# A depthwise-convolution and MLP kernel: the first tap's product on GpSimd, and other half steps for the visits

## Chip, core and metric

The kernel runs on one core of a Trainium2 chip. The metric is the device time of one execution in microseconds (us); lower is better. A core has five engines that run their own instruction queues in order: TensorE (PE in the profile; its weight loads PEld), VectorE (DVE), ScalarE (ACT), GpSimd (POOL) and SyncE (SP). DMAs are issued by SP, ACT and POOL queues.

## What is computed

With S = 2048 positions, D = 448 channels and F = 1792, all in float32:

```python
xn = layernorm(q)
# branch A: short causal convolution of k (4 taps), times v, long causal convolution, gate
k_shift = sum(k_pad[:, t:t + S] * shift_k[:, 3 - t] for t in range(4))
kv = k_shift * v
y = irfft(rfft(kv, 2 * S) * rfft(ssm_k, 2 * S))[:S] + kv * ssm_D
A = xn * y
# branch B: dense, Mish, dense
B = mish(xn @ w1 + b1) @ w2
out = q + A + B
```

## The kernel before

**Branch B sets the rhythm.** The 2048 positions are 8 chunks c of 256, the 1792 hidden channels 7 pairs p of 128-wide blocks; (c, p) is pair i = 7c + p. Each pair takes two half steps. In the even one, s = 2i, TensorE runs `g1_mm(i)` (line 556, 22 matmuls with split operands); in the odd one `mish(i)` (ScalarE, line 564; then `split`, whose line 98 is a ScalarE cast to `ach` and line 99 a VectorE subtraction to `acl`), and TensorE runs `g2_mm(i - 2)` (lines 588 to 590, 12 matmuls, which accumulate a chunk in two PSUM tiles). When a chunk's last pair is through, `g2_evac` (line 595, VectorE, two operations) empties those two tiles into Q; the next chunk's first `g2_mm` writes the same two. For chunk 1 that is half steps 32 and 33, for chunk 2 half steps 45 and 47.

**Branch A lies between.** The long convolution is a Fourier transform in two stages. The first stage works on 8 groups g of 256 positions, once for the filter h and once for kv. A "visit" at half step t is `f1_mm` (line 166, 16 small matmuls into the PSUM tiles pq and pr), then `f1_fold` (ScalarE copies pr, line 172; VectorE adds and subtracts, line 176, twice), then, three half steps later, `f1_out` (line 187, two DMAs to the scratch tensors Dh or Dkv). From half step 60 on the second stage ("octets", lines 255 to 321) reads Dh and Dkv back.

**kv itself** is made on VectorE by `taps(g, u)` for u = 0 to 3, spread over the half steps ahead of the visit: u = 0 is one product k times tap (line 209, 128x896); u = 1 and 3 are two half products (lines 212 and 214) and an addition (219); u = 2 has its product made on GpSimd by `taps_pool` (line 202) and only added here (219); after u = 3 the sum is multiplied with v (222). `taps_pool(g + 1, 2)` is put behind the visit of g, ahead of its fold; it begins with a VectorE memset of one element (line 201) which makes GpSimd wait until VectorE has come that far. The k tiles come from `k_load` (line 192, SP, four buffers), v from `v_load` (196).

**LayerNorm of chunks 3 to 7**: `nt_stats` at half step NT_STATS[c] (27, 41, 53, ... ; ScalarE lines 478 to 480, GpSimd 481 and 482, and a DMA to MR, line 486, on POOL), `nt_row` (line 489: SP loads MR, broadcast to all partitions), `nt_norm` (line 495, VectorE, a pair of operations) and `nt_split` (ScalarE 502, VectorE 503), twice for each chunk.

**What sets the order.** The program is written out half step by half step: `at(t, ...)` puts work ahead of the matmuls of half step t, `after(t, ...)` behind them, in the order of registration; every engine, and every DMA queue, then takes its own part of that one order strictly in turn. H_AT and KV_AT hold the half steps of the visits of h and kv. For kv, with d the distance to the visit before:

```python
    for g, t in enumerate(KV_AT):
        d = t - (KV_AT[g - 1] if g else t - 6)
        at(t - d - (3 if g > 1 else 2), k_load, g)
        at(t - d - 1, v_load, g)
        for u in range(4):
            after(t - (2 if g else 1) - d + d * u / 4, taps, g, u)
        at(t, f1_mm, KV, g, "kv")
```

Of the kernel before, what the change touches and what calls it, by code (L numbers as in the profile page):

```python
# [14 lines left out]
S, D, F = 2048, 448, 1792  # L15
# [7 lines left out]

G2_LAG = 2
H_HEAD = 1
H_AT = {2: 6, 3: 9, 0: 12, 4: 16, 5: 20, 6: 26, 7: 32}
KV_AT = (24, 29, 34, 39, 44, 50, 56, 60)
POOL_H = {20: (0, 2)}
OCT_AT = (66, 3)
I2_AT = {100: ((6, 7, 0, 1), 92, (95, 97, 98, 99), (0, 2, 0, 1)),  # L30
# [20 lines left out]
def tile_kernel(ctx: ExitStack, tc, q, qT, k, v, sk, hT, sD, head, w1, w2, c_g, c_gi, c_i2, out):  # L51
    nc = tc.nc
    V = nc.vector
# [67 lines left out]
    def dv(n=1):  # L121
        for _ in range(n):
            if drip:
                drip.pop(0)()
# [4 lines left out]
    def at(slot, fn, *args):  # L129
        plan.setdefault(int(slot), []).append((fn, args))  # L130
# [7 lines left out]
    skb = sp1.tile([128, 4, D], F32, name="skb")  # L138
    HT, KR, VT, KV, PP, PS, ST, SD = {}, {}, {}, {}, {}, {}, {}, []

    def xt():
        return sp1.tile([128, 2, D], F32, name="x", bufs=7)
# [61 lines left out]
    def taps(g, u):  # L204
        if (g, u) in PP:
            o = PP.pop((g, u))
        elif u % 2 == 0:
            o = xt()
            V.tensor_mul(o, KR[g - u // 2], skb[:, u:u + 1].to_broadcast([128, 2, D]))
        else:  # L210
            o = xt()
            V.tensor_mul(o[:, 0], KR[g - (u + 1) // 2][:, 1], skb[:, u])
            dv()
            V.tensor_mul(o[:, 1], KR[g - u // 2][:, 0], skb[:, u])
        dv()
        if u == 0:
            KV[g] = o
        else:
            V.tensor_add(KV[g], KV[g], o)  # L219
            dv()  # L220
        if u == 3:
            V.tensor_mul(KV[g], KV[g], VT.pop(g))
            dv()
# [430 lines left out]

    for g, t in H_AT.items():
        if g != H_HEAD:
# [10 lines left out]
    for g in range(-2, 0):  # L667
        at(12, k_load, g)
# [7 lines that stand above are left out]
        if g + 1 < NO:  # L676
            after(t, taps_pool, g + 1, 2)
        after(t, f1_fold, g, "kv")
        (at if t % 2 or g == NO - 1 else after)(t + (3 if g < NO - 1 else 2), f1_out, Dkv, g, "kv")
# [216 lines left out]
```

## Time and profile before

| | |
|---|---|
| median of 3 runs | 357.84 us (356.28 to 359.15) |
| the profiled execution: time, span | 356.18 us, 354.4 us |
| mean granted TensorE clock | 0.998 |
| busy PE, PEld | 349.8 us (99%), 288.6 us (81%) |
| busy DVE, ACT, POOL | 282.1 us (80%), 160.7 us (45%), 72.6 us (20%) |
| the stretch 48 to 186 us: PE, DVE, POOL busy | 138.00, 119.08, 31.74 us |

A row of the profile's groups gives line, engine, operation, out<-in tiles, shapes, count, then busy time and mean duration in ns, then the idle time ahead of it and what ended most of it. A row in order of time starts with the start and the duration in us ("x2" puts two operations together); what stands in brackets is the idle time ahead. The duration of a VectorE row is a little longer than the distance to the next start: two rows of 1.09 that don't depend on each other start 1.00 apart.

### The profile page before, as it was taken

The page shows a single profiled execution, that of the slowest core. Times are in us where ns is not written, and L with a number is a line of the kernel's source. Part 1 is how long each engine was busy: PE and PEld are TensorE (multiplying, and loading weights), DVE is VectorE, ACT ScalarE, POOL GpSimd, SP SyncE. Part 2 cuts the span into 40 slices and gives each one's busy share as a digit, 9 for nine tenths or more (in the row PEclk, how much of TensorE's full clock was granted, in tenths as well). Part 3 has the DMA queues.
Part 4 walks back from the last instruction along what each step waited for, and adds up shares of the span by engine and source line. Part 5 has one row for each costly group of instructions (what it writes and reads, how often), then busy time and mean ns, then how long its engine had stood idle before and what let it go on. Part 6 is the DMA issues. An engine that isn't in the chain of part 4 may idle for free.

```text
span 354.4 us, 7525 instructions
## 1 busy us (share of the span) xinstructions
PE 349.8 (99%) x3098; PEld 288.6 (81%) x3098; DVE 282.1 (80%) x375; ACT 160.7 (45%) x310; POOL 72.6 (20%) x85
## 2 busy tenths in 40 slices
PE   8999999999999999999999999999999999999996
PEld 2988888888888989889887568658757699979795
DVE  5899748998999998979539869868985963788943
ACT  5967552347343643364232732423724333354480
POOL 3046002822220250212000120110310116040030
PEclk9999999999999999999999999999999999999999
DMA  7999977848769356652969489679756467989076
GB/s 251 366 339 353 401 277 182 338 131 236 212 178 314 128 150 176 219 163 36 298 187 365 149 307 298 229 243 372 263 144 254 105 173 261 407 334 277 25 116 143
DMA packets 30835, 83.27 MB, mean 235 GB/s; under 512 B 3153, under 2 KB 15954, under 8 KB 30802
## 3 DMA queue, kind: packets, MB, share of 16 engines
q1 hardware_dynamic: 21986, 47.78, 39.8%
q0 software_dynamic: 4928, 22.95, 20.4%
q10 hardware_dynamic: 3888, 12.08, 12.5%
q8 instruction: 24, 0.39, 0.4%
q14 instruction: 9, 0.07, 0.1%
HBM read 54.34 MB, written 28.45 MB: 234 GB/s over the span
## 4 chain that ended last, share of the span: by engine, by line
PE 97%; DMA 1%; SPq 0%; DVE 0%; issue 0%
PE pg L556 24%; PE pg L590 13%; PE pg L588 13%; PE pg L589 13%; PE pa L556 6%; PE pq L556 5%; PE pq L166 4%; PE pa L310 3%; PE pr L556 3%; PE pr L255 3%; PE pq L255 3%; PE pp L556 2%; PE pa L255 1%; DMA x<-in_head_dram 1%; PE pp L364 1%; PE pb L556 1%
## 5 line engine op out<-in xcount | busy, mean ns | idle before, releaser
L588 PE MATMUL pg<-w2h,ach 128*128 128x448 f32 x222 | 80.7, 363 | 0.0
L590 PE MATMUL pg<-w2h,acl 128*128 128x448 f32 x222 | 80.6, 363 | 0.0
L589 PE MATMUL pg<-w2l,ach 128*128 128x448 f32 x222 | 80.5, 362 | 0.0
L99 DVE TENSOR_TENSOR acl<-a,ach 128x512 fp32r<-128x512 f32 x56 | 38.9, 694 | 33.0 <-ACT ach L98 32.8
L556 PE MATMUL pg<-XH,w1h 128*128 128x256 f32 x264 | 52.7, 283 | 0.0
L564 ACT ACTIVATE a<-pg,b1t 128x256 f32<-128x256 f32 x66 | 27.8, 472 | 51.8 <-PE pg L556 40.9
L556 PEld LDWEIGHTS pg<-XH,w1h 128*128 128x128 f32 x264 | 41.3, 188 | 8.2 <-issue 6.3
L588 PEld LDWEIGHTS pg<-w2h,ach 128*128 128x128 f32 x222 | 41.6, 187 | 4.4 <-issue 1.4
L589 PEld LDWEIGHTS pg<-w2l,ach 128*128 128x128 f32 x222 | 41.7, 188 | 2.4
L590 PEld LDWEIGHTS pg<-w2h,acl 128*128 128x128 f32 x222 | 41.7, 188 | 2.4
L556 PE MATMUL pg<-XL,w1h 128*128 128x256 f32 x264 | 42.9, 277 | 0.0
L176 DVE TENSOR_TENSOR st<-pq,st 128x896 f32<-128x896 f32 x32 | 34.9, 1089 | 4.8 <-ACT st L172 4.2
L98 ACT CAST ach<-a 128x512 fp32r<-128x512 f32 x56 | 34.8, 621 | 8.2 <-PE pg L589 6.7
L556 PEld LDWEIGHTS pg<-XL,w1h 128*128 128x128 f32 x264 | 35.9, 188 | 0.0
L556 PE MATMUL pg<-XH,w1l 128*128 128x256 f32 x198 | 33.5, 278 | 0.0
L202 POOL TENSOR_TENSOR x<-kr,skb 128x896 f32<-128x896 f32 x8 | 17.0, 2128 | 72.1 <-PE pr L166 25.7
L321 POOL DMA_DIRECT2D E<-qe x14 | 8.8, 631 | 92.7 <-ACT qe L264 92.7
L556 PEld LDWEIGHTS pg<-XH,w1l 128*128 128x128 f32 x198 | 27.6, 188 | 0.0
L219 DVE TENSOR_TENSOR x<-x 128x896 f32<-128x896 f32 x24 | 26.2, 1091 | 1.1 <-POOL x L202 0.4
L172 ACT COPY st<-pr 128x896 f32<-128x896 f32 x16 | 14.5, 908 | 15.9 <-PE pr L166 14.7
L564 ACT ACTIVATE a<-pa,b1t 128x256 f32<-128x256 f32 x16 | 6.7, 472 | 20.8 <-PE pa L556 20.7
L166 PE MATMUL pq<-x,con 32*64 32x448 f32 x128 | 15.9, 560 | 0.1
(191 smaller groups left out, 645.8 us busy)
## 6 DMA issues: line engine op xcount, KB each, us to landing
Dkv<-st ACTq DMA_DIRECT2D x16, 448.0 KB, 5.5
ah<-Dh SPq DMA_DIRECT2D x8, 896.0 KB, 8.4
av<-Dkv SPq DMA_DIRECT2D x8, 896.0 KB, 9.6
e<-E POOLq DMA_DIRECT2D x8, 896.0 KB, 7.3
E<-qe POOLq DMA_DIRECT2D x14, 448.0 KB, 7.1
kr<-in_k_dram SPq DMA_DIRECT2D x10, 448.0 KB, 6.0
Dh<-st ACTq DMA_DIRECT2D x10, 448.0 KB, 6.9
x<-in_v_dram SPq DMA_DIRECT2D x8, 448.0 KB, 6.3
```

The source lines that it names most:

```text
L98: nc.scalar.copy(h, raw)
L99: V.tensor_sub(l, raw, h)
L166: nc.tensor.matmul(ps[h][64 * jj:64 * jj + 64, b, :D], f1[rg:rg + 32], x[rg:rg + 32, jj], start=True, stop=True, tile_position=(rg, 64 * jj))
L176: f(st[:, n], e, st[:, 1])
L202: nc.gpsimd.tensor_mul(o, KR[g - u // 2], skb[:, u:u + 1].to_broadcast([128, 2, D]))
L219: V.tensor_add(KV[g], KV[g], o)
L255: nc.tensor.matmul(bk(p, r)[32 * t:32 * t + 32, :D], g[rs, t, c], a[rs, t], start=True, stop=True, tile_position=(64 * r, 32 * t))
L556: nc.tensor.matmul(ps[n], l, r, start=all(m[0] != n for m in seq[:n_]), stop=all(m[0] != n for m in seq[n_ + 1:]))
L564: nc.scalar.activation(a[:, n], ps[n], AF.Mish, bias=b1t[:, 2 * p + n:2 * p + n + 1])
L588: nc.tensor.matmul(ps, ah[:, n, cs], w2h[:, f], start=f == 0, stop=False)
L589: nc.tensor.matmul(ps, ah[:, n, cs], w2l[:, f], start=False, stop=False)
L590: nc.tensor.matmul(ps, al[:, n, cs], w2h[:, f], start=False, stop=f == NF - 1 or (f == NF - 3 and jj == 1 and c == NCHUNK - 1))
```

## The change

GpSimd makes the product of u = 0 in place of VectorE for every g but 1; the visits of kv go from 24, 29, 34, 39, 44, 50, 56, 60 to 24, 30, 36, 42, 46, 52, 56, 60; h's last group goes from 32 to 38. The new products on GpSimd have no memset ahead of them.

```diff
-H_AT = {2: 6, 3: 9, 0: 12, 4: 16, 5: 20, 6: 26, 7: 32}
-KV_AT = (24, 29, 34, 39, 44, 50, 56, 60)
+H_AT = {2: 6, 3: 9, 0: 12, 4: 16, 5: 20, 6: 26, 7: 38}
+KV_AT = (24, 30, 36, 42, 46, 52, 56, 60)
@@ def taps(g, u) @@
         elif u % 2 == 0:
             o = xt()
-            V.tensor_mul(o, KR[g - u // 2], skb[:, u:u + 1].to_broadcast([128, 2, D]))
+            (V if u or g == 1 else nc.gpsimd).tensor_mul(o, KR[g - u // 2], skb[:, u:u + 1].to_broadcast([128, 2, D]))
```

What stands in GpSimd's queue between the MR store of chunk 3 (the L486 just ahead of the first row) and the visits of g = 3 to 5, with the statistics of chunk 4 (lines 481, 482, 486) in the middle; - is before, + is after:

```order
-L202 TENSOR_TENSOR x<-kr,skb 128x896 x3
+L209 TENSOR_TENSOR x<-kr,skb 128x896
+L202 TENSOR_TENSOR x<-kr,skb 128x896
+L209 TENSOR_TENSOR x<-kr,skb 128x896
+L202 TENSOR_TENSOR x<-kr,skb 128x896
+L209 TENSOR_TENSOR x<-kr,skb 128x896
 L481 TENSOR_SCALAR ve<-bst 128x2
 L482 TENSOR_TENSOR mv<-ve,mhalf 128x2
 L486 DMA MR<-mv 128x2x2
-L202 TENSOR_TENSOR x<-kr,skb 128x896 x2
+L202 TENSOR_TENSOR x<-kr,skb 128x896
+L209 TENSOR_TENSOR x<-kr,skb 128x896
```

Ahead of the statistics there were the second products (L202) of g = 2, 3 and 4; now there are the first and second of g = 2 and 3 and the first of g = 4, and the second product of g = 4 has moved behind the statistics, with the first of g = 5 right behind it.

VectorE's queue around the emptying of chunk 1's PSUM tiles (L595) at half step 32, in before:

```order
L99 TENSOR_TENSOR acl<-a,ach 128x512
L201 MEMSET x 1x1
L176 TENSOR_TENSOR st<-pq,st 128x896 x2
L219 TENSOR_TENSOR x<-x 128x896
L212 TENSOR_TENSOR x<-kr,skb 128x448
L214 TENSOR_TENSOR x<-kr,skb 128x448
L219 TENSOR_TENSOR x<-x 128x896
L222 TENSOR_TENSOR x<-x 128x896
L99 TENSOR_TENSOR acl<-a,ach 128x512
L595 TENSOR_TENSOR qt<-pg_753,qt 128x448
L595 TENSOR_TENSOR qt<-pg_757,qt 128x448
```

and after (the first row are the L99 of half steps 27 and 29; the first row above is that of 29):

```order
L99 TENSOR_TENSOR acl<-a,ach 128x512 x2
L212 TENSOR_TENSOR x<-kr,skb 128x448
L214 TENSOR_TENSOR x<-kr,skb 128x448
L219 TENSOR_TENSOR x<-x 128x896
L201 MEMSET x 1x1
L176 TENSOR_TENSOR st<-pq,st 128x896 x2
L99 TENSOR_TENSOR acl<-a,ach 128x512
L219 TENSOR_TENSOR x<-x 128x896
L595 TENSOR_TENSOR qt<-pg_753,qt 128x448
L595 TENSOR_TENSOR qt<-pg_757,qt 128x448
```

Ahead of L595 there was the end of g = 2's work (u = 2 and 3); now there is its beginning (u = 1, which waits for the first product from GpSimd, and u = 2), with the fold of g = 1's visit at 30 in between.

SP's queue from the k load of g = 5 on (in after; L489 are the two MR rows of chunk 4):

```order
L192 DMA kr<-in_k_dram 128x896
L196 DMA x<-in_v_dram 128x896
L489 DMA con<-MR 128x256
L615 DMA out_dram<-qt 128x896
L489 DMA con<-MR 128x256
L426 DMA qt<-in_q_dram 128x896
L192 DMA kr<-in_k_dram 128x896
L196 DMA x<-in_v_dram 128x896
L192 DMA kr<-in_k_dram 128x896
```

The second L192 here is the k load of g = 6, which stood ahead of both L489 in before and now stands behind them.

## The prediction

> **What bounds the kernel now.** I read four views in this order: the page's busy times, the busy times of the stretch in which the visits lie, TensorE's instructions in order of time, and then what VectorE and GpSimd do to each other. Page, engines, then the stretch 48 to 186 us (columns: length, and busy time of PE, PEld, DVE, ACT, POOL with counts; clock; DMA):
>
> ```profile
> PE 349.8 (99%) x3098; PEld 288.6 (81%) x3098; DVE 282.1 (80%) x375; ACT 160.7 (45%) x310; POOL 72.6 (20%) x85
> ```
> ```profile
> 48.00:186.00 138.00, 138.00 (x1069) 122.47 (x1060) 119.08 (x160) 60.66 (x124) 31.74 (x22) 1.00 0.65 196
> ```
>
> TensorE is busy in all 138.00 us, at granted clock 1.00. As ends of matmuls are modelled, I check that by starts, which hide nothing:
>
> ```profile
> 105.65 0.52 PE L556 MATMUL pg<-XH,w1h 128*128 128x256 f32 x3
> ...
> 108.15 0.36 PE L588 MATMUL pg<-w2h,ach 128*128 128x448 f32 x1
> ...
> 110.55 0.51 PE L556 MATMUL pg<-XH,w1h 128*128 128x256 f32 x3
> ...
> 113.15 0.59 PE L166 MATMUL pq<-x,con 32*64 32x448 f32 x2
> ...
> 114.09 0.47 PE L588 MATMUL pg<-w2h,ach 128*128 128x448 f32 x1
> ```
>
> An even half step (22 matmuls of line 556) takes 2.50 us, an odd one (12 of lines 588 to 590) 2.40; a visit of line 166 takes 0.94 and makes its neighbours 0.2 longer (2.60 for 2.50 ahead of it): 1.2 in all. The same steps, without a gap, run from 48 to 185 us. So nothing that relieves VectorE can make this stretch shorter; the change can only leave TensorE fed or starve it. VectorE, with 119.08 of 138 us, is the engine that feeds it, in order.
>
> **What the change removes and adds.** Groups by line (count | busy us, mean ns):
>
> ```profile
> L202 POOL TENSOR_TENSOR x<-kr,skb 128x896 f32<-128x896 f32 x8 | 17.0, 2128 | 72.1 <-PE pr L166 25.7
> L219 DVE TENSOR_TENSOR x<-x 128x896 f32<-128x896 f32 x24 | 26.2, 1091 | 1.1 <-POOL x L202 0.4
> L209 DVE TENSOR_TENSOR x<-kr,skb 128x896 f32<-128x896 f32 x8 | 8.7, 1084 | 0.0
> ```
>
> Seven of the eight L209 leave VectorE: 7 x 1.0 us there (rows of 1.09 start 1.0 apart). GpSimd gets 7 x 2.13 = 14.9 us, priced by L202, the same operation and shape; it has room (31.74 of 138). No instruction is added on TensorE, ScalarE or SP.
>
> The question is what a GpSimd product costs VectorE beside it. All eight L202 of before start behind a memset just ahead of the fold's two L176, which read PSUM and one SBUF tile. The new products have no such memset: they start when k is there and GpSimd is free, beside L219, L212, L222 and L99, which read two SBUF tiles. The trace has a few such meetings. GpSimd's L455, by duration (min/median/max ns) and in order of time, then VectorE:
>
> ```profile
> L455 POOL TENSOR_SCALAR xn<-qt,mv,rstd x4: 1853/2324/2776, 24.8 to 66.0; 128x448 f32<-128x448 f32 x4
> ```
> ```profile
> 62.73 2.77 POOL L455 TENSOR_SCALAR xn<-qt,mv,rstd 128x448 f32<-128x448 f32 x1
> ```
> ```profile
> 62.74 1.10 DVE L219 TENSOR_TENSOR x<-x 128x896 f32<-128x896 f32 x1
> 63.84 1.05 DVE L99 TENSOR_TENSOR acl<-a,ach 128x512 fp32r<-128x512 f32 x1
> 64.81 0.61 DVE L212 TENSOR_TENSOR x<-kr,skb 128x448 f32<-128x448 f32 x1
> ...
> 67.12 1.49 DVE L222 TENSOR_TENSOR x<-x 128x896 f32<-128x896 f32 x1
> ```
>
> L455 is 0.92 us above its shortest, the length of the L219 beside it; then L99 takes 1.05 (L495, of the same shape, takes 0.69 below), and at 67.12 L222 1.49 for L219's 1.09. So they wait for each other, and an operation that reads 448 elements costs VectorE 0.36 to 0.40 us, all at its start: L212 inside the same span is not slowed. For L202 itself there is one meeting:
>
> ```profile
> 145.35 2.13 POOL L202 TENSOR_TENSOR x<-kr,skb 128x896 f32<-128x896 f32 x1 [13.31 <-issue]
> ```
> ```profile
> L495 DVE TENSOR_TENSOR xn<-xn,con x10: 683/692/766, 103.0 to 180.9; 128x512 f32<-128x512 f32 x10
> ```
> ```profile
> 147.26 1.49 DVE L495 TENSOR_TENSOR xn<-xn,con 128x512 f32<-128x512 f32 x2
> ```
>
> The longest of ten L495 (766 for 692 ns) is in the pair at 147.26, 1.91 us into that product: it was let go 1.91 + 0.07 = 1.98 us after the product's start. So the **price of a product that meets such operations** lies between 0.4 us (L455's, an operation with a quarter of the reads) and 2.13 (its whole length); below nothing I exclude, since no row beside GpSimd is shorter. I take 2.0, the row of the same operation. Against 1.0 saved, that is a net loss of 1.0 us of VectorE for each product, and 2.0 at the spot where it falls.
>
> [...]
>
> **Where it reaches TensorE.** Half-step starts of after are those of before, less 1.2 for each visit that has moved behind them. Three places miss their start.
>
> Place 1, half step 33. Its L588 overwrites the PSUM that L595 empties; one visit fewer lies ahead of it (24, 26, 30 for 24, 26, 29, 32).
>
> ```profile
> 88.03 0.84 POOL L486 DMA_DIRECT2D MR<-mv  x1 [0.29 <-POOL mv L482]
> ```
> ```profile
> 88.09 0.69 DVE L99 TENSOR_TENSOR acl<-a,ach 128x512 fp32r<-128x512 f32 x1 [1.20 <-ACT ach L98]
> 96.04 1.15 DVE L595 TENSOR_TENSOR qt<-pg,qt 128x448 f32<-128x448 f32 x2
> ```
> ```profile
> 97.19 0.36 PE L588 MATMUL pg<-w2h,ach 128*128 128x448 f32 x1
> ```
>
> TensorE wants it at 97.19 - 1.2 = 96.0. Chunk 3's statistics are not moved, so GpSimd is free for g = 2's first product at 88.9, as now. VectorE's queue, from L99 at 88.1: L212 88.7, then the product holds it from 89.2 to 91.2; L214, L219 until 92.9; fold to 95.0; L99 to 95.6; g = 3's first product, next in GpSimd's queue behind L202 (2.13 from 92.95), holds from 95.6 to 97.6; L219 to 98.6; the first L595 ends 99.2. **Stall 3.3 us** (0.5 at price 0: the chain then waits for GpSimd at 91.1 and ends 96.5).
>
> Place 2, the visit at 46. Statistics of chunk 4 stay at half step 41, but g = 4's second product (L202), ahead of them in GpSimd's queue in before, now stands behind them. ScalarE's and GpSimd's rows for one such round:
>
> ```profile
> 119.20 0.37 PE L588 MATMUL pg<-w2h,ach 128*128 128x448 f32 x1
> ```
> ```profile
> 120.80 0.57 ACT L478 ACTIVATE a<-qt 128x448 f32<-128x448 f32 x1
> ...
> 124.04 0.19 ACT L480 ACTIVATION_READ_ACCUMULATOR a<-qt,mv 128x1 f32 x1
> ```
> ```profile
> 156.94 0.19 POOL L481 TENSOR_SCALAR ve<-bst 128x2 f32<-128x2 f32 x1 [9.45 <-ACT a L480]
> 157.21 0.72 POOL L482 TENSOR_TENSOR mv<-ve,mhalf 128x2 f32<-128x2 f32 x1
> 158.22 0.78 POOL L486 DMA_DIRECT2D MR<-mv  x1 [0.29 <-POOL mv L482]
> ```
>
> Half step 41 begins at 119.20 - 1.2 = 118.0; the statistics begin 1.6 later, take 3.4, GpSimd's part 2.1, the product 2.1: done at 127.2. From there VectorE has L219 (1.0), L99 (0.6) and L212, L214, L219, L222 (3.4 together, as each waits for the one ahead): 132.2. The visit is due at 118.0 + 13.4 (half steps 41 to 45 and the visit at 42) = 131.4. That is 0.8 late at price 0. At 2.0, g = 5's first product follows at once in GpSimd's queue and takes its 2.0 out of the middle of this chain: **stall 2.8 us**. Place 1's stall moves both sides alike.
>
> Place 3, the visit at 56.
>
> ```profile
> con<-MR SPq DMA_DIRECT2D x10, 128.0 KB, 5.2
> kr<-in_k_dram SPq DMA_DIRECT2D x10, 448.0 KB, 6.0
> ```
> ```profile
> 158.37 0.59 PE L166 MATMUL pq<-x,con 32*64 32x448 f32 x2
> ```
>
> The due time is 26.9 behind the visit at 46 (ten half steps, two visits; 158.37 is its place in before, with as many visits ahead). All times from the visit at 46: VectorE ends its first L495 pair for chunk 4 at 8.9 (L99, two L595, three operations of g = 5, fold, L99, L219, the pair). k's load for g = 6 now stands in SP's queue behind the second MR row of chunk 4, which waits for that pair; in before it stood ahead. So k is issued near 9.7, lands 6.0 later at 15.7, and the product is done at 17.9. Then L219 1.0, L503 0.6, fold 2.2, L219 1.0, L99 0.6, last four 3.4: 26.8 at price 0, just on time. At 2.0, L212 and L214 too stand behind the product: 28.2, late by 1.3; and by 3.3 if g = 7's first product, which waits for chunk 5's statistics, gets in ahead of the last L222, a matter of 0.3 us. I take the middle: **stall 2.3 us**. The visit at 60 then has a microsecond left.
>
> Elsewhere there is cover. g = 0's first product falls near 53 us, and what it takes from VectorE it takes ahead of this wait:
>
> ```profile
> 60.61 1.09 DVE L176 TENSOR_TENSOR st<-pq,st 128x896 f32<-128x896 f32 x1 [1.09 <-ACT st L172]
> ```
>
> Sum: 3.3 + 2.8 + 2.3 = **8.4 us**. What I cost at nothing: h's visit at 38 needs the banks of 36's fold, which by the same queue ends 2 us ahead of it; g = 1's product stays on VectorE. The stores to Dh and Dkv move by up to six half steps, but the octets read them past 60. The profiled execution took 356.18: 356.2 + 8.4 = **364.6 us** (+2.4%). The runs' median, 357.84, is 1.7 above that execution, so medians may stand as much higher.
>
> **Rivals.** (a) The price is L455's, 0.4 us, or nothing. Then the order alone costs 0.5 + 0.8, and 0.4 for a product at places 1 and 2 each: 356.2 + 2.1 = 358.3 us. For it: L212 inside L455. Against it: the L495 row. (b) Not slower: VectorE's 7 us of relief and the wider gaps (6 half steps for 5) absorb all three places. That needs a price under 1.0, VectorE's break-even, and GpSimd ready 0.8 us earlier than its rows say, at place 2 above all: 356.2 us. Against it: at price 0 the statistics alone make place 2 late, and TensorE has no idle time to win back. (c) Delays add up: at 2.13, with 3.3 at place 3 and loads behind the stalls late too, 366 to 369. That the products might not move is excluded by the order of instructions.
>
> **Chances.** Forecast 0.6 (362 to 367), (a) 0.23, (b) 0.1, (c) 0.07. To hold 8 in 10 the range leaves out most of (b) and half of (c): 356.8 to 368. A change under 1% (3.6 us) can hardly be told from none here. Faster by more 0.02; within 0.32: (a) and (b); slower 0.66.
>
> **What would show it.** VectorE rows of lines 99, 212, 219 or 222 at 2 to 3 us beside L209 of GpSimd; TensorE busy for 8 us less than its stretch; gaps ahead of L588 at half step 33 (about 96 us) and ahead of L166 at 46 and 56. If those VectorE rows keep 0.69 and 1.09, the price was wrong and (a) holds. If TensorE has no gaps, it is (b).

## The result, and the profile after

| | before | after |
|---|---|---|
| median of the runs, us | 356.82 (6 runs, 356.28 to 359.15) | **374.25** (6 runs, 373.51 to 374.91) |
| ratio to before | | **1.048**, 95% interval 1.044 to 1.051 |
| profiled execution, us (span) | 356.18 (354.4) | 373.51 (371.7) |

The change costs 17.4 us. The direction was forecast, the amount was not: 364.6 was predicted and the range ended at 368.0. The page of after, engines, granted clock, and the chain that ended last:

```profile
PE 355.6 (96%) x3098; PEld 292.2 (79%) x3098; DVE 287.8 (77%) x368; ACT 160.7 (43%) x310; POOL 88.3 (24%) x92
PEclk9999999999899998997899999999999999999999
PE 75%; DVE 12%; DMA 4%; ACT 3%; issue 2%; POOL 1%; ACTq 1%; SPq 1%; POOLq 0%; DVEq 0%
```

TensorE is busy in 96% instead of 99% of the span, VectorE stands in the chain with 12%, and **the clock row has digits below 9 in three places, which before has nowhere**. VectorE is busy for 287.8 us with 7 instructions fewer than in before, where it was 282.1. The stretch 48 to 186 us and the waits of TensorE (us in total, times, longest):

```profile
48.00:186.00 138.00, 127.34 (x932) 111.29 (x931) 117.21 (x143) 55.11 (x114) 46.29 (x29) 0.95 0.55 169
```
```profile
PE pq L166 <- DVE x L222: 7.3, 2, 3.7
PE pg L588 <- DVE qt L595: 3.4, 1, 3.4
```

Three waits, 10.7 us in all, where the prediction put them. TensorE's rows at the three places, in order of time (start, duration, idle before):

```profile
100.28 0.71 PE L588 MATMUL pg<-w2h,ach 128*128 128x448 f32 x1 [3.40 <-DVE qt L595]
...
141.23 1.01 PE L166 MATMUL pq<-x,con 32*64 32x448 f32 x2 [3.72 <-DVE x L222]
...
173.24 1.01 PE L166 MATMUL pq<-x,con 32*64 32x448 f32 x2 [3.54 <-DVE x L222]
```

What stands behind each wait: GpSimd's new products, and VectorE's rows that began beside them.

```profile
88.93 2.12 POOL L209 TENSOR_TENSOR x<-kr,skb 128x896 f32<-128x896 f32 x1
96.11 2.53 POOL L209 TENSOR_TENSOR x<-kr,skb 128x896 f32<-128x896 f32 x1
...
134.17 2.12 POOL L209 TENSOR_TENSOR x<-kr,skb 128x896 f32<-128x896 f32 x1
158.62 2.46 POOL L209 TENSOR_TENSOR x<-kr,skb 128x896 f32<-128x896 f32 x1 [11.24 <-DMA kr<-in_k_dram]
170.15 2.08 POOL L209 TENSOR_TENSOR x<-kr,skb 128x896 f32<-128x896 f32 x1
```
```profile
88.87 2.74 DVE L99 TENSOR_TENSOR acl<-a,ach 128x512 fp32r<-128x512 f32 x1 [2.87 <-ACT ach L98]
...
96.63 2.96 DVE L219 TENSOR_TENSOR x<-x 128x896 f32<-128x896 f32 x1
...
134.25 3.00 DVE L219 TENSOR_TENSOR x<-x 128x896 f32<-128x896 f32 x1 [1.30 <-POOL x L202]
...
159.03 2.53 DVE L214 TENSOR_TENSOR x<-kr,skb 128x448 f32<-128x448 f32 x1
...
169.63 3.56 DVE L222 TENSOR_TENSOR x<-x 128x896 f32<-128x896 f32 x1
```

L99 normally takes 0.69, L219 and L222 1.09, L214 0.62 (rows of before). They are 2.05, 1.87, 1.91, 1.91 and 2.47 us too long. The first four have the forecast price of 2.0, the fifth is dearer. Of the other two new products, g = 4's at 114.41 made a pair of L495 last 3.22 for 1.42, and g = 0's at 49.46 ran beside a fold, whose two L176 kept their 2.22.

But the rows of TensorE above are also too long themselves: 0.71 for 0.36, 1.01 for 0.59. Windows of 3.41 us around each wait (length, busy time of PE, PEld, DVE, ACT, POOL with counts; then granted clock, DMA):

```profile
96.87:100.28 3.41, 0.01 (x2) 0.04 (x1) 3.41 (x3) 1.46 (x3) 1.78 (x1) 1.00 0.49 108
100.28:103.69 3.41, 3.41 (x9) 3.06 (x10) 3.34 (x5) 0.00 (x0) 0.00 (x0) 0.50 0.96 238
137.83:141.24 3.41, 0.01 (x2) 0.01 (x2) 3.34 (x6) 0.00 (x0) 0.00 (x0) 1.00 0.93 257
141.24:144.66 3.42, 3.42 (x24) 2.02 (x25) 3.32 (x6) 0.91 (x1) 0.00 (x0) 0.50 0.31 127
168.55:171.96 3.41, 1.15 (x6) 0.73 (x4) 3.38 (x2) 0.43 (x1) 3.09 (x3) 1.00 0.70 135
171.96:175.38 3.42, 2.14 (x18) 0.74 (x19) 3.31 (x5) 0.23 (x1) 0.27 (x1) 0.50 0.47 135
175.38:178.79 3.41, 3.41 (x18) 3.41 (x18) 3.35 (x5) 0.67 (x1) 2.11 (x1) 0.50 0.16 30
```

After each wait the granted clock is 0.50 for one or two such windows. The matmuls in them take nearly twice their time: the half step behind the first wait 4.08 us for 2.40, the other two 1.67 and 2.68 longer. **The clock costs 1.68 + 1.67 + 2.68 = 6.0 us, and the prediction has no term for it.** Waits (3.5 + 3.8 + 3.6 = 10.9 by the starts of the half steps) and clock make 16.9 of the 17.3 us between the two spans.

### The profile page after: what moved, and what is told of

Same layout as the page of the kernel before. It is cut to its first block, busy times and chain, and to the rows that moved or that the text cites. A ratio compares the mean times of both kernels' runs of the same rounds, so it can differ in the third digit from the quotient of the medians.

```text
span 371.7 us, 7535 instructions
## 1 busy us (share of the span) xinstructions
PE 355.6 (96%) x3098; PEld 292.2 (79%) x3098; DVE 287.8 (77%) x368; ACT 160.7 (43%) x310; POOL 88.3 (24%) x92
## 4 chain that ended last, share of the span: by engine, by line
PE 75%; DVE 12%; DMA 4%; ACT 3%; issue 2%; POOL 1%; ACTq 1%; SPq 1%; POOLq 0%; DVEq 0%
PE pg L556 15%; PE pg L590 9%; PE pg L588 9%; PE pg L589 9%; PE pa L556 6%; PE pq L556 5%; DVE x L219 3%; PE pq L166 3%; PE pa L310 3%; PE pr L556 3%; DMA kr<-in_k_dram 3%; PE pr L255 3%; PE pq L255 3%; DVE st L176 2%; PE pp L556 2%
## 5 line engine op out<-in xcount | busy, mean ns | idle before, releaser
L588 PE MATMUL pg<-w2h,ach 128*128 128x448 f32 x222 | 81.2, 366 | 3.4 <-DVE qt L595 3.4
L99 DVE TENSOR_TENSOR acl<-a,ach 128x512 fp32r<-128x512 f32 x56 | 41.1, 734 | 39.0 <-ACT ach L98 38.8
L564 ACT ACTIVATE a<-pg,b1t 128x256 f32<-128x256 f32 x66 | 27.8, 472 | 61.8 <-PE pg L556 49.8
L556 PE MATMUL pg<-XH,w1h 128*128 128x256 f32 x264 | 54.3, 290 | 0.0
L556 PEld LDWEIGHTS pg<-XH,w1h 128*128 128x128 f32 x264 | 42.4, 194 | 11.0 <-issue 8.4
L588 PEld LDWEIGHTS pg<-w2h,ach 128*128 128x128 f32 x222 | 42.1, 190 | 6.6 <-issue 3.6
L556 PE MATMUL pg<-XL,w1h 128*128 128x256 f32 x264 | 43.3, 279 | 0.0
L176 DVE TENSOR_TENSOR st<-pq,st 128x896 f32<-128x896 f32 x32 | 34.9, 1089 | 7.6 <-ACT st L172 7.0
L556 PEld LDWEIGHTS pg<-XL,w1h 128*128 128x128 f32 x264 | 36.5, 191 | 0.0
L556 PE MATMUL pg<-XH,w1l 128*128 128x256 f32 x198 | 34.4, 283 | 0.0
L219 DVE TENSOR_TENSOR x<-x 128x896 f32<-128x896 f32 x24 | 29.9, 1247 | 2.4 <-POOL x L202 1.5
L556 PEld LDWEIGHTS pg<-XH,w1l 128*128 128x128 f32 x198 | 28.6, 195 | 0.0
L202 POOL TENSOR_TENSOR x<-kr,skb 128x896 f32<-128x896 f32 x8 | 17.0, 2125 | 42.8 <-DVE x L201 36.9
L166 PE MATMUL pq<-x,con 32*64 32x448 f32 x128 | 17.5, 612 | 8.2 <-DVE x L222 7.3
L209 POOL TENSOR_TENSOR x<-kr,skb 128x896 f32<-128x896 f32 x7 | 16.0, 2287 | 26.3 <-DMA kr<-in_k_dram 26.3
```

Source lines behind the costliest of these rows:

```text
L99: V.tensor_sub(l, raw, h)
L166: nc.tensor.matmul(ps[h][64 * jj:64 * jj + 64, b, :D], f1[rg:rg + 32], x[rg:rg + 32, jj], start=True, stop=True, tile_position=(rg, 64 * jj))
L176: f(st[:, n], e, st[:, 1])
L202: nc.gpsimd.tensor_mul(o, KR[g - u // 2], skb[:, u:u + 1].to_broadcast([128, 2, D]))
L556: nc.tensor.matmul(ps[n], l, r, start=all(m[0] != n for m in seq[:n_]), stop=all(m[0] != n for m in seq[n_ + 1:]))
L564: nc.scalar.activation(a[:, n], ps[n], AF.Mish, bias=b1t[:, 2 * p + n:2 * p + n + 1])
```

## The experiments

All times are medians. Before, run on the same chip beside them, had 357.06 to 357.20 (7 runs each time); the three kernels of "the clock by itself" ran once each, beside one run of before with 357.67.

### The two halves of the change

**Half steps alone.** Seven products stay on VectorE.

```diff
-            (V if u or g == 1 else nc.gpsimd).tensor_mul(o, KR[g - u // 2], ...)
+            V.tensor_mul(o, KR[g - u // 2], ...)
```

> The half steps of the change alone; all first products stay on VectorE, as in before. Theory (a GpSimd product holds VectorE off for 2.0 us, and the new order is late by itself): no VectorE row longer than 1.5 us; no wait at half step 33 above 0.5 us; the visit at 46 about 0.6 us late (the second product of g = 4 behind the statistics), the visit at 56 late by 2 to 3.5 us, because VectorE has to make what GpSimd made; 359 to 361 us, 362 if the gap at 56 reaches 3.4 us and the clock halves for 3.4 us behind it. Rival (the half steps are harmless, the products do it all): 356.5 to 357.5 us. Rival (the half steps do it all): 370 us or more.

Measured: 365.33 us, ratio 1.024 (1.019 to 1.029), above what was expected. The waits of TensorE, then VectorE's and SP's rows ahead of the longer one, at 56:

```profile
PE pq L166 <- DVE x L222: 8.8, 2, 6.4
```
```profile
154.53 1.09 DVE L209 TENSOR_TENSOR x<-kr,skb 128x896 f32<-128x896 f32 x1 [5.69 <-DMA kr<-in_k_dram]
```
```profile
144.34 0.32 SPq L489 DMA_DIRECT2D con<-MR  x1
...
145.38 1.52 SPq L192 DMA_DIRECT2D kr<-in_k_dram  x1
```

With the product in VectorE's own queue, the late k of g = 6 (issued right behind the second row of chunk 4's statistics, as forecast) holds VectorE itself for 5.69 us, and the visit waits 6.4. The other wait, 2.4 us, is at 46. So the half steps cost 8.3 us without any product on GpSimd, more than rival (a) gave them. (The profile is of the slowest of the four runs, 367.68.) A spell of half clock follows the wait at 56 and none the one at 46.

**Products alone**, at the old half steps:

```diff
-            V.tensor_mul(o, KR[g - u // 2], ...)
+            (V if u or g == 1 else nc.gpsimd).tensor_mul(o, KR[g - u // 2], ...)
```

> The seven products on GpSimd alone, at the half steps of before. Theory: VectorE rows of lines 99, 212, 219, 222 or 495 with 2.0 us too much beside most of the seven products, but the order of before leaves each wait of TensorE under 2 us, so no half clock: 359 to 362 us. Rival (the half steps do it all): 356.5 to 357.5. Rival (products alone do it all, whatever the half steps): above 368.

Measured: 361.68 us, ratio 1.013 (1.011 to 1.016), clock 1.00 from 48 to 190 us. The waits of TensorE are short; a third one, of 0.8 us ahead of L556 at 77 us, makes them 3.6 in all:

```profile
PE pg L588 <- DVE qt L595: 1.5, 2, 1.3
PE pq L166 <- DVE x L222: 1.3, 1, 1.3
```

Either half alone is a loss, and 8.3 + 4.6 = 12.9 is less than the 17.4 of both. It is not the waits that grow: the two halves have 8.8 and 3.6 us of them in their profiles, both together 10.9. What grows is the half clock, which costs 1.8 us with the half steps alone (from the visit at 56 to the next L588 it is 5.21 us for 3.44), nothing with the products alone, and 6.0 with both.

### What a product takes from VectorE

**Memset for the product.** GpSimd writes the same tile and reads nothing, so the first tap is left out of the result.

```diff
-            (V if u or g == 1 else nc.gpsimd).tensor_mul(o, KR[g - u // 2], ...)
+            if u or g == 1:
+                V.tensor_mul(o, KR[g - u // 2], ...)
+            else:
+                nc.gpsimd.memset(o, 0.0)
```

> The kernel after, but GpSimd fills the seven tiles with zeros (a write of the same 128x896 that reads nothing) in place of the product: the first tap is left out. Theory (it is the reads of the product that hold VectorE off): no VectorE row longer than 1.5 us beside L211 to L214's memsets; what is left is the order, waits of about 0.5 us at 46 and 0.5 to 1 us at 56; 357.5 to 359 us. Rival (any work of GpSimd holds VectorE off, or the order alone starves TensorE): VectorE rows 0.8 us or more too long, or above 364 us.

Measured: 361.03 us, ratio 1.011 (1.009 to 1.013). The waits of TensorE (line 225 is line 222 of after), and GpSimd and VectorE at place 1:

```profile
PE pq L166 <- DVE x L225: 2.4, 1, 2.4
```
```profile
89.07 0.87 POOL L212 MEMSET x<- 128x896 f32 x1
```
```profile
89.20 0.69 DVE L99 TENSOR_TENSOR acl<-a,ach 128x512 fp32r<-128x512 f32 x1 [3.03 <-ACT ach L98]
```

L99 has its 0.69 again, and the waits at places 1 and 3 are gone. At place 1 the two rows held up in after are 2.05 and 1.87 us too long for a wait of 3.5, so that wait hangs on the hold (the memset is also done sooner, 0.87 us for 2.12). At place 3 the memset also needs no k, so this run can't part the hold from the late load (see "Place 3" below). Place 2 stays with 2.4 us; the window that holds the wait has 1.02 us of work, and one of half clock follows it, which costs 1.7 us (from the visit to the next L591, line 588 of after, it is 5.15 us for 3.44). I had put place 2 at 0.6 to 0.8 without a hold, so the total is 2 us above my expectation.

**Half a product.** GpSimd makes 128x448 of the first product, VectorE the other 128x448.

```diff
-                nc.gpsimd.tensor_mul(o, KR[g], ...)
+                nc.gpsimd.tensor_mul(o[:, 0], KR[g][:, 0], skb[:, 0])
+                V.tensor_mul(o[:, 1], KR[g][:, 1], skb[:, 0])
```

> After, with GpSimd making only the first half (128x448) of each of the seven products and VectorE the other half. Theory A (GpSimd holds VectorE off for nearly its whole length): GpSimd's pieces take about 1.1 us and the VectorE rows beside them are 1.0 too long instead of 2.0. Waits of TensorE between those with 2.0 (3.5, 3.8, 3.6) and those without a hold (0, 2.4, 0), about 2.0, 3.2 and 2.0, and half clock after the one at 46 alone: 357 + 7.2 + 1.7 = 366, range 363 to 368. Theory B (each meeting has a fixed price, whatever the length): rows 2.0 too long, VectorE has half a product more per visit, 374 or above.

Measured: 371.55 us (369.36 to 371.99). GpSimd's rows, then VectorE's beside them (line 223 is 219 of after):

```profile
88.61 1.16 POOL L212 TENSOR_TENSOR x<-kr,skb 128x448 f32<-128x448 f32 x1
...
94.84 1.60 POOL L212 TENSOR_TENSOR x<-kr,skb 128x448 f32<-128x448 f32 x1
```
```profile
88.54 1.78 DVE L99 TENSOR_TENSOR acl<-a,ach 128x512 fp32r<-128x512 f32 x1 [2.33 <-ACT ach L98]
...
95.35 2.03 DVE L223 TENSOR_TENSOR x<-x 128x896 f32<-128x896 f32 x1
```

The rows are 1.09 and 0.94 too long: half the work, half the hold, as theory A has it. The total missed its range by 3.5 us: VectorE's half of the product waits in order for k, as in the kernel with the half steps alone, the waits came to 9.2 instead of 7.2, and two spells of 6.8 us at half clock followed where I had allowed for one of 3.4.

So in these runs a product, 2.08 to 2.56 us long, held up the VectorE rows that it met (L99, L214, L219, L222 and a pair of L495) by 1.80 to 2.05 us, once by 2.47; half a product, 1.16 and 1.60 us long, by 1.09 and 0.94; and the memset, 0.87 us long, left L99 at its 0.69.

### The clock by itself

Before, with n additions on VectorE ahead of the last product of g = 7; TensorE waits nowhere else between 48 and 186 us in this kernel.

```diff
+            if g == 7:
+                for _ in range(n):
+                    V.tensor_add(o, KV[g], VT[g])
```

n = 2: 

> The kernel before with two extra additions (128x896, 1.0 us each, result unused) on VectorE ahead of g = 7's last product, so that TensorE waits at kv's visit of half step 60 and nowhere else. The product ends about 0.9 us before it is needed, so the wait should be about 1.1 us. Theory A (TensorE runs at half clock in the next 3.4 us whenever it was busy less than half of a 3.4 us window): 1.1 us cannot bring a window under half, clock 1.00, 357 + 1.1 = 358.2. Theory B (only a window without any work, thus a wait of 3.4 us or more, lowers the clock): the same, 358.2.

n = 4: 

> The same with four additions: a wait of about 3.1 us at half step 60. Theory A: a window under half busy unless the wait falls evenly on two windows, so most likely one spell of 3.4 us at half clock, which costs 1.7 us: 357 + 3.1 + 1.7 = 361.9 (360.2 if split evenly, with both windows above half). Theory B: no window is empty, clock 1.00, 360.2.

n = 6: 

> The same with six additions: a wait of about 5.1 us. Theory A: at least one spell at half clock whatever the phase, 3.4 or 6.8 us long: 363.8 to 365.5. Theory B: a spell only where a whole window falls into the wait, half the phases: 362.1 or 363.8, and the window before the spell has no matmul in it.

Measured: 357.71, 362.94 and 365.79 us, with waits of 1.3, 3.6 and 5.8 us. The windows at n = 4, in which the wait lies:

```profile
168.12:171.53 3.41, 1.33 (x7) 0.91 (x5) 3.31 (x4) 0.46 (x1) 0.00 (x0) 1.00 0.96 330
171.53:174.95 3.42, 1.93 (x17) 0.53 (x18) 3.07 (x5) 0.03 (x1) 0.00 (x0) 0.50 0.61 204
174.95:178.36 3.41, 3.41 (x17) 3.41 (x18) 2.18 (x2) 0.88 (x1) 0.00 (x0) 0.50 0.33 135
178.36:181.77 3.41, 3.41 (x22) 3.26 (x22) 0.69 (x1) 1.46 (x3) 0.00 (x0) 1.00 0.13 28
```

With 1.3 us the clock stays at 1.00. Against the profile of before, TensorE's starts are 1.4 us later behind this wait than ahead of it, so the wait costs its length and no more; the two single runs (357.71, and 357.67 of before) are too few to show that in the total. With 3.6 us no window is empty: TensorE is busy for 1.33 of 3.41 us in the window that holds most of the wait, and the next two windows run at 0.50. Theory B (only an empty window counts) falls; theory A fits here, as the window with the wait at n = 2 has 2.10 us of work. At n = 6 the first of three windows has 0.86 us of work, and again two at 0.50 follow. The spell is longer than I expected: the window in which TensorE was busy for 1.93 us did not bring the clock back, the one with 3.41 did. By the same comparison the starts behind the wait are 6.1 us later at n = 4, for a wait of 3.6, and 7.6 later at n = 6, for 5.8: the clock costs about 2.5 and 1.8 us there. Both totals are above what was expected, by 1.0 and 0.3 us, as the waits were 0.5 and 0.7 longer too.

**Filler matmuls.** After, with 13 matmuls whose result is unused ahead of half steps 33, 46 and 56, so that TensorE is not idle for the whole wait.

```diff
+            if s == 33:
+                fill_pe(13)
...
+        if t in (46, 56):
+            at(t, fill_pe, 13)
```

> The kernel after, with 13 matmuls of 0.2 us each (2.6 us, into the bank pq that the next visit overwrites) put ahead of the three places where TensorE waits, half steps 33, 46 and 56; the waits themselves stay. Theory (the clock halves because TensorE stood idle for 3.4 us): idle is now under 1.3 us at each place, the clock stays at 1.00, and the 6.0 us of half clock go: 367.5 to 369 us. Rival (the slow clock has another cause, the load of the whole stretch for one): the clock record keeps its three spells, 373 to 375 us.

Measured: 370.25 us (367.75 to 372.06), which is 4.0 below after although TensorE does 39 matmuls more, and 1.3 above the range that was expected. Two of the three spells are gone, worth 1.68 + 2.68 = 4.4; the one at 46 remains, behind a window with 1.62 us of work:

```profile
99.15:102.56 3.41, 2.63 (x14) 2.46 (x14) 3.38 (x6) 0.00 (x0) 0.00 (x0) 1.00 0.99 228
136.70:140.11 3.41, 1.62 (x16) 1.14 (x20) 3.34 (x5) 0.00 (x0) 0.00 (x0) 1.00 0.87 284
140.11:143.52 3.41, 3.41 (x24) 2.01 (x25) 3.31 (x6) 0.91 (x1) 0.00 (x0) 0.50 0.30 124
```

The waits are no shorter (at place 1, 2.6 us of matmuls and 0.8 of waiting for 3.4), so the clock is a cost of its own beside them. In one of the four runs the granted clock was 1.000 throughout; it is the fastest, at 367.75.

### Place 3: k's load

k's load for g = 6 is issued three half steps earlier, ahead of chunk 4's rows; once in the kernel with the half steps alone, once in after.

```diff
-        at(t - d - (3 if g > 1 else 2), k_load, g)
+        at(t - d - (6 if g == 6 else 3 if g > 1 else 2), k_load, g)
```

Half steps alone: 

> The retimed kernel with all first products on VectorE (half steps of after, products of before), and k's load for g = 6 issued three half steps earlier, ahead of chunk 4's rows of statistics in SP's queue. Theory A (the wait of 6.4 us at 56 comes from k, which lands late because its load stands behind the second row): that wait and its half-clock spell are gone, the 2.4 us at 46 stay: 357.1 + 2.4 = 359.5, or 361.2 with a half-clock spell after 46. Theory B (the wait at 56 is VectorE's backlog from chunk 4's normalisation): it stays at 4 us or more, 363 or above.

After: 

> After, with k's load for g = 6 issued three half steps earlier, products on GpSimd as in after. Theory A (as predicted, place 3 is late by k's late load and by what two products take from VectorE): the product of g = 6 runs some microseconds earlier, the hold of g = 7's product in front of the last L222 stays, so the wait at 56 falls from 3.6 to about 2, and the spell of 6.8 us at half clock to 3.4 or none: 374.2 - 1.6 - 1 to 2.7 = 370 to 371.6. Theory B (the holds alone make it late): 373.5 to 375. Theory C (k alone): wait gone, 368.

Measured, half steps alone: 360.48 us, ratio 1.010 (1.007 to 1.013), 4.9 below the same kernel with the late k. The waits of 8.8 in all become

```profile
PE pq L166 <- DVE x L222: 3.1, 2, 2.4
```

2.4 at 46 and 0.7 at 56, with the clock at 1.00. Theory A, shown. In after: 368.91 us (368.31 to 370.12), 5.3 below after.

```profile
PE pq L166 <- DVE x L222: 5.5, 2, 4.2
```

At 56 (170.66 us) TensorE no longer waits; the shorter of the two waits, 1.3 us, is at the visit at 60 (183.00), and no half clock follows it. So the wait at 56 goes, as theory C has it, where theory A left about 2; the total is 0.9 above C's 368 and below A's 370 to 371.6. With k in time the hold that A left in front of the last L222 does not reach TensorE. Places 1 and 2 keep their waits (3.4 and 4.2) and their half clock.

### Place 2: a store in ScalarE's queue

With half steps alone place 2 waits 2.4 us, with no product on GpSimd and k in time. ScalarE's rows show where it begins (early-k kernel; half step 41 begins at 118.26 on TensorE):

```profile
114.43 1.24 ACTq L187 DMA_DIRECT2D Dkv<-st  x2
115.77 4.09 ACTq L187 DMA_DIRECT2D Dh<-st  x2
119.91 0.84 ACT L564 ACTIVATE a<-pg,b1t 128x256 f32<-128x256 f32 x2 [4.86 <-DVE x L209]
...
121.30 0.57 ACT L478 ACTIVATE a<-qt 128x448 f32<-128x448 f32 x1
```

h's visit has moved from 32 to 38 and takes its two stores with it, from half step 35 to 41. There they stand right behind kv's two, take 4.09 us to issue instead of the usual 1.24, and half step 41's Mish (L564), then the statistics (L478), start 1.4 us late (the L209 that L564's row names as releaser ended at 119.20; L564 starts as the stores' issue ends). To test it, SP issues them.

```diff
-        at(t + (2 if t < 12 else 3), f1_out, Dh, g, "h", nc.gpsimd if t < 12 else nc.scalar)
+        at(t + (2 if t < 12 else 3), f1_out, Dh, g, "h", nc.gpsimd if t < 12 else nc.sync if g == 7 else nc.scalar)
```

Half steps alone, early k: 

> The retimed kernel with early k (all first products on VectorE), and the two stores of h's last group (half step 41) issued by SP instead of ScalarE. Theory A (behind kv's two stores these two take ScalarE's queue 4.1 us instead of 1.2, so that Mish of half step 41, then chunk 4's statistics, GpSimd's second product and the visit at 46 are each about 1.5 us late): the statistics start 1.5 us earlier, the wait at 46 falls from 2.4 to about 0.9, as the prediction had it without a hold (0.8): 360.5 - 1.5 = 359.0. Theory B (the wait at 46 comes from the place of the statistics alone): 2.4 stays, 360.5.

After: 

> After, with the two stores of h's last group issued by SP instead of ScalarE, nothing else changed. Theory A (as above): the wait at 46 falls from 3.8 to between 2.3 and the forecast 2.8, the waits at 33 and 56 stay (3.5 and 3.6): 374.2 - 1.0 to 1.5 = 372.7 to 373.2, and 1.7 less, 371.0 to 371.5, if the shorter wait lets no window of TensorE fall under half. Theory B: no change, 374.

Measured, half steps alone: 358.81 us, ratio 1.0047 (1.0029 to 1.0065). The waits, and where the statistics now begin, 1.60 us into half step 41 instead of 3.04:

```profile
PE pq L166 <- DVE x L222: 1.6, 2, 0.9
```
```profile
119.87 0.57 ACT L478 ACTIVATE a<-qt 128x448 f32<-128x448 f32 x1
```

Shown for that kernel: 2.4 becomes 0.9. In after the same edit gives 372.12 us (371.6 to 374.41), 2.1 less, with the wait at 46 down from 3.7 only to 3.2. Most of the 2.1 is not place 2 but the clock at place 1: its wait is 3.4 us as in after, but here it falls on two windows with 1.59 and 1.84 us of work, and no half clock follows either. The two runs with this mean clock, 0.986, took 371.6 and 371.8 us, the other two, at 0.982 and 0.980, 372.4 and 374.4. The statistics are earlier there too (2.50 us into half step 41 in after, 1.97 with the edit), but k's load for g = 5 now stands behind the two stores in SP's queue: it is issued 4.1 us into half step 41, where in after it was issued 1.5 us ahead of it. So the product of g = 5 waits 0.98 us for k, misses the L219 and lands on the L99 behind it. SP's row and GpSimd's:

```profile
126.24 0.37 SPq L192 DMA_DIRECT2D kr<-in_k_dram  x1
```
```profile
132.88 2.12 POOL L209 TENSOR_TENSOR x<-kr,skb 128x896 f32<-128x896 f32 x1 [0.98 <-DMA kr<-in_k_dram]
```

No version beats before. The best of these, 358.81, is still 1.6 us above it, and before has no wait of TensorE in this stretch left to remove.

## Why the prediction was wrong

- **What bounds the kernel: right.** TensorE had nothing to gain from 48 to 186 us; no kernel here is faster than before.
- **The price of a product, 2.0 us between bounds of 0.4 and 2.13: right.** Five VectorE rows are 1.87 to 2.47 us too long, one of them above the upper bound. Rivals (a) and (b), which needed a low price, are refuted. Rival (c), 366 to 369 by delays that add up, has no term for the clock either.
- **Where it reaches TensorE: right in place, low in size.** Of 10.9 us measured, 8.4 were forecast. Place 1: 3.3 forecast, 3.5 measured. Place 2: 2.8 forecast, 3.8 measured; the missing 1.0 is a step named and costed at nothing, "the stores to Dh and Dkv move by up to six half steps". In after the statistics begin 2.50 us into half step 41 where the sum had 1.6, behind the stores:

```profile
121.89 3.15 ACTq L187 DMA_DIRECT2D Dh<-st  x2
```

  I looked at who reads the stored data, not at the queue that issues the store. That this is the cause is shown with the half steps alone; in after the test made the statistics only 0.5 us earlier and moved k's load with them. Place 3: 2.3 forecast as the middle between 1.3 and 3.3, 3.6 measured; the upper case happened, as the row of L222 with 3.56 us beside g = 7's product at 170.15 shows. That the upper case fits so well in size owes something to luck, as two shifts cancel that the sum did not have: k was issued 10.8 us behind the visit at 46 and its product began 6.6 later, for 9.7 and 6.0 in the sum, and the half clock behind 46 put off the due time by the same 1.7. The row is 0.4 longer than the product's own length explains, and whose time this is stays open.
- **The step that failed: the sum, which has no term for the clock.** It adds waits at a TensorE that afterwards runs as before, and 6.0 us of half clock came on top. With the waits as measured and the clock at 1.00 the sum would have been 356.2 + 10.9 = 367.1, inside the range. Before never drops below 1.00 in this stretch, but it does once, at its very end, where TensorE runs out of work in the middle of a window:

```profile
349.39:352.80 3.41, 1.68 (x14) 1.51 (x12) 1.41 (x3) 0.00 (x0) 0.00 (x0) 1.00 0.59 173
352.80:354.40 1.60, 0.00 (x0) 0.00 (x0) 0.00 (x0) 0.00 (x0) 0.00 (x0) 0.50 0.00 0
```

  A window with 1.68 of 3.41 us of work is followed by 0.50. So the mean clock of 0.998 had a row behind it that one could have looked up; a forecast of gaps should have asked what the clock does after them, and kept that open in the range.

The spells here last 3.41 and 6.83 us, and their starts fall on one grid within each run. The window ahead of a spell need not be empty: the one with 1.33 us of work at n = 4 was followed by 0.50 too. Over the kernels here, windows at full clock with at most 1.33 us of work were followed by half clock and none with 1.75 or more was; from these numbers, about half a window, I estimate that a wait from about 1.7 us up can lower the clock, and each of my forecast stalls (3.3, 2.8, 2.3 us) is longer than that. The shortest that did was 2.4 us (memset for the product, a window with 1.02 us of work); 2.4 us in the early-k kernel, on two windows with 2.36 and 2.11, did not.

## What to carry to other kernels

Price a wait of a saturated matmul engine twice, once for its length and once for what the profile shows of the clock after it: here waits of about 3.5 us cost 1.7 to 2.7 us more (once 0.1, where two windows shared the wait), a wait of 1.3 us nothing more. When a step moves, follow each instruction that it issues into the queue where it now stands, the stores that nobody is waiting for as well. And an engine that is three quarters idle (GpSimd, 24% busy in after) is no free place for work that holds up the busy engine: the seven products that left VectorE gave it 7 us and took about 2 us each from the six rows or pairs that they met.

## What the runs showed of the hardware

- In the profiled execution of each kernel here, the granted clock of TensorE changes between about 88 and 190 us only on a grid of 3.413 us, from 1.00 to 0.50 or back (after: the spells begin at 100.28, 141.24 and 171.96 us, the later two 12 and 21 steps behind the first). Of its windows at full clock, the 13 with 0.00 to 1.33 us of work were each followed by half clock, and none with 1.75 us or more was. One with 1.62 us (filler matmuls) was followed by it and one with 1.59 (after with the stores on SP) was not; before's last full window, with 1.68 us, was followed by it too. Busy times are modelled, so from these numbers I can only estimate the limit as near half a window.
- Eight windows at half clock that were not full (0.08 to 2.80 us of work) were followed by half clock again, the 14 full ones (3.41 us) by 1.00. The same wait cost different amounts where it fell differently on the grid: behind 3.4 us at place 1 the spell is 3.4 us long in after, 6.8 in after with the early k, and there is none in after with the stores on SP: 1.7, 2.7 and 0.1 us of cost. This does not explain all of the scatter: two runs of the half steps alone with the same mean clock, 0.991, took 363.94 and 366.68 us.
- Four store issues in a row on ScalarE: the second pair takes 3.15 us in after, 4.10 with the memset for the product and 4.09 with the half steps alone and the early k, where a pair alone mostly takes 1.24 (at most 2.26, from 48 to 185 us in these three and before). Why was not tested.
